# A softcap attention with a maxout layer behind it: another order in the hand-written list of work

## The chip, the cores and the metric

The kernel runs on one core of one Trainium2 chip. The core has five engines with a stream of instructions each: TensorE (PE, matmuls; its weight loads are a stream of their own, PEld), VectorE (DVE), ScalarE (ACT), GpSimd (POOL) and SyncE (SP). POOL and SP issue DMAs here. An engine runs its own instructions in order and waits for the others by semaphores. The metric is device microseconds for one execution; less is better. Several runs are made, and their median counts.

## The reference

```python
q, k, v: 8 x 12 x 448 x 64 (batch, heads, tokens, head size); cap = 30
scores = (q @ k^T) / 8
scores = cap * tanh(scores / cap)
attn = softmax(scores)                          # over the last axis
x = (attn @ v)  as rows of tokens: 3584 x 768
h1, h2 = x @ w1, x @ w2                         # w1, w2: 768 x 1024
out = maximum(h1, h2) @ w_out                   # w_out: 1024 x 768; out: 3584 x 768
```

## The kernel before

**What is computed.** No maximum is subtracted before the exponential, since tanh bounds the scores at 30; the scores are computed with k along the partitions, so that the exponents are already the operand of the matmul with v. The maxout layer is rewritten: max(h1, h2) @ w_out = relu(x (w1 − w2)) @ w_out + x (w2 w_out). `wd_sb` holds w1 − w2, `wm_sb` holds w2 w_out, and both are made at the start of each execution. All matmul operands are bf16.

**Units.** A pair `i` (0 to 47) is two heads, a quad `t` (0 to 23) is two pairs, so a batch is three quads. For a quad the steps are: transposed q and k (`X`/`XC` on PE and DVE for the first five quads; `cr t`, a DMA transpose that SP issues, L475, for the others), scores `S i j` (three blocks of keys, L509 to L514, two halves of 64 rows each), tanh `T i j` on ACT (L519), the left-over 64 keys `L`/`TL`/`EL`, exponents `E i j0 j1` on ACT (L536), sums of exponents `A` and `B` on DVE (L548, L553) and `Y` on PE, their inverse `Y1`, `Y2`, `Y3` on DVE, values `VL` and `V` on PE, and the normalisation `N t u` on DVE, which writes `xT` (u = 0 in one instruction, L618; u = 1 in two, L621).

**The layer.** It is computed in 120 groups, each one PSUM bank: `O g bank` opens a group, `M x y n` issues n pairs of half-matmuls (rows 0 to 63 for group x, rows 64 to 127 for group y), `M x x n` issues n full ones, `ev g` evicts it on DVE (relu, L666, or a copy, L702), and `eva g` does the copy on ACT (L700). A group has its two halves one after the other, and both add into the same bank. So between them stands a hand-over: `H g` puts a nop on DVE, `Hs g` puts it on SP (L652 to L655). The nop waits for the last half-matmul that the group had so far, and the first half-matmul of its other half waits for the nop (L646 to L648). `st b t` issues two output DMAs from SP (L676 to L681). POOL loads q, k, v and the weights (`lq`, `lk`, `lv`, `lw1`, `lw2`, `lwo`). `W`, `WC`, `P` and `PC` make `wm_sb`; `sub` makes `wd_sb`; `D` are matmuls that warm PE.

**The order.** It is a text, `ORDER` (lines 9 to 201): a list of steps that a loop at the end carries out one by one (L742 to L745). No scheduler moves anything, so each engine runs its instructions in the order in which the list issues them. The list decides nothing about time between engines: an instruction waits for what it reads, for buffers, and for what stands ahead of it on its engine.

**Buffers.** The transposed q and k have two buffers (`QB`), their rows two (`KB`). So `cr t` waits for the last scores of quad t − 2 as well as for its own loads: `cr 16`, say, writes the buffer of quad 14, whose last scores are `S 29 2`. The score tiles in PSUM are also reused: the values of a quad lie in one of them until `N` has read both parts.

Of the kernel before, what the change touches and what calls it, by code (L numbers as in the profile page):

```python
# [21 lines left out]
S 5 0; X 6 0; E 4 0 3; T 5 0; EL 2; Y1 1; Y2 1; PC 2 1; Y3 1; N 1 1; N 1 0; XC 6; X 7 2; W 4 1; S 5 2; S 5 1;
X 8 0; P 3 1 3; WC 4; XC 8; PC 3 1; T 5 1; T 5 2; OP 4 0 1; P 4 0 2; OP 0 1 0; P 0 1 3; S 6 0; S 6 1; W 5 3;
P 0 1 1; P 4 0 6; P 0 1 4; E 5 0 2; T 6 1; T 6 0; E 5 2 3; XC 7; sub 2 0; WC 5; sub 4 0; PC 4 0; sub 0 0; PC 0 1;
OP 5 1 3; P 5 1 4; S 6 2; L 3; Y 2 1; T 6 2; TL 3; E 6 0 3; VL 2; V 2 1 0 1; V 2 0 0 3; V 2 1 1 3; S 7 0; P 5 1 4;
OP 5 0 0; P 5 0 8; Y1 2; Y2 2; Y3 2; N 2 0; N 2 1; A 3 0 1; A 3 0 2; PC 5 1; PC 5 0; T 7 0; EL 3; lk 9 0; lq 11 0;
lv 3 1; lq 9 0; lw1 1; lw1 3; lq 10 0; lk 12 1; lv 3 0; lw1 5; lk 10 0; lk 11 0; lk 11 1; lk 10 1; S 7 2; O 0 1;
M 0 -1 2; S 7 1; M 0 -1 4; O 1 2; M 1 -1 1; T 7 2; T 7 1; Hs 0; M 1 -1 1; S 8 1; M 1 -1 1; M 1 0 3; S 8 0; X 9 3;
OP 4 1 0; P 4 1 4; sub 1 0; sub 3 0; XC 9; T 8 1; E 7 0 2; T 8 0; E 7 2 3; P 4 1 4; L 4; O 2 3; M 2 0 3; S 8 2;
M 2 1 3; A 3 1 1; B 3 1; PC 4 1; ev 0; B 3 0; Hs 2; TL 4; T 8 2; O 3 0; M 3 1 3; M 3 2 1; S 9 0; M 3 2 2; T 9 0;  # L30
E 8 0 3; ev 1; A 3 1 2; sub 5 0; cr 5; Hs 3; O 4 1; M 4 2 1; VL 3; V 3 0 0 3; Y 3 2; V 3 1 0 3; M 4 2 2; S 9 1;
M 4 3 3; lk 13 0; lk 13 1; lv 4 1; lv 4 0; lv 5 3; lv 5 0; lq 13 0; lq 15 0; lq 12 0; lk 12 0; lk 15 1; Y1 3;
Y2 3; Y3 3; ev 2; Hs 4; O 5 2; M 5 3 3; M 5 4 3; T 9 1; EL 4; ev 3; N 3 0; N 3 1; Hs 5; O 6 3; M 6 4 3; M 6 5 2;
# [172 lines left out]
def kernel(  # L206
# [21 lines left out]
    P = 128  # L228
# [550 lines left out]
```

## Time and profile before

| | before |
|---|---|
| median of 3 runs | 328.59 us |
| fastest and slowest run | 327.98 and 329.32 us |
| span of the profiled execution | 326.9 us |
| moved by DMA | 46.28 MB, 142 GB/s in the mean |
| TensorE clock granted | 0.9 or more in each of 40 slices |
| stores (SP), number and median to landing | 54, 4.5 us |

The profiled execution's span is 1.7 us under the median of the runs; it is counted from its first to its last instruction. In the profile, a row of the timeline is: start, duration, engine, line, operation, output and input names, and, in brackets, the idle time ahead of it and what ended it. An engine name with a q (SPq, DVEq) is the engine's own queue of waits and DMA issues. A nop of a hand-over shows as an EVENT_SEMAPHORE of L654.

### The profile page before, as it was taken

What the parts mean: (1) busy time and instruction counts of PE and PEld (TensorE: products, weight loads), DVE (VectorE), ACT (ScalarE), POOL (GpSimd) and SP (SyncE); (2) the same over time, 40 slices, a digit from 0 to 9 for tenths busy, and PEclk for the clock granted to TensorE, in tenths of its full rate; (3) what the DMA queues carried; (4) which work ended last, traced back from release to release, by engine and by line L of the source; (5) the groups of instructions that cost most, each with busy time, mean ns of one, the idle gap of its engine ahead of it and who ended that gap; (6) DMA issues with size and microseconds to landing.
All of it is one profiled execution on the core that took longest, in us unless ns stands there. A gap on an engine that the chain in (4) does not pass through costs nothing.

```text
span 326.9 us, 9772 instructions
## 1 busy us (share of the span) xinstructions
PE 320.2 (98%) x4138; PEld 184.5 (56%) x4138; DVE 240.1 (73%) x422; ACT 281.1 (86%) x278; POOL 162.2 (50%) x237
## 2 busy tenths in 40 slices
PE   7999999999999999999999999999999999999994
PEld 3454545545656664565565565556466556557662
DVE  3346899987997778987897788968878779773201
ACT  5999999999999999999999999999999999921120
POOL 7357584568772772764774474478448311000000
PEclk9999999999999999999999999999999999999999
DMA  8999999899999999999999999999999963013033
GB/s 179 174 202 185 269 256 112 92 140 116 221 188 98 134 182 191 102 99 175 163 176 108 208 114 181 128 140 182 183 116 101 201 156 45 2 50 98 0 98 96
DMA packets 134508, 46.28 MB, mean 142 GB/s; under 512 B 112321, under 2 KB 129473, under 8 KB 134465
## 3 DMA queue, kind: packets, MB, share of 16 engines
q0 software_dynamic: 94592, 25.02, 78.3%
q1 hardware_dynamic: 39424, 19.99, 31.1%
q8 instruction: 32, 0.52, 0.6%
q10 hardware_dynamic: 448, 0.66, 0.5%
q14 instruction: 12, 0.09, 0.1%
HBM read 47.78 MB, written 11.01 MB: 180 GB/s over the span
## 4 chain that ended last, share of the span: by engine, by line
PE 93%; DMA 3%; POOL 1%; DVE 1%; issue 0%
PE mm L645 61%; PE s L514 9%; PE s L606 9%; PE mm L431 5%; DMA w2b<-in_moe_w_dram 3%; PE s L528 2%; PE s L600 2%; PE mm L573 2%; PE mm L640 1%; POOL kqs L321 1%; PE mm L458 1%; PE mm L566 1%; PE mm L416 0%; DVE xT L621 0%; POOL w2b L366 0%; DVE xT L618 0%
## 5 line engine op out<-in xcount | busy, mean ns | idle before, releaser
L519 ACT ACTIVATE e<-s 128x896 bf16<-128x896 f32 x144 | 125.5, 927 | 5.7 <-PE s L514 5.2
L536 ACT ACTIVATE e<-e 128x1792 bf16<-128x1792 bf16 (+2 forms) x72 | 122.7, 1709 | 0.0
L645 PE MATMUL mm<-wo_sb,gT 64*128 64x384 bf16 x864 | 115.2, 323 | 0.0
L645 PE MATMUL mm<-wm_sb,xT 64*128 64x384 bf16 x648 | 102.2, 323 | 0.0
L645 PE MATMUL mm<-xT,wd_sb 64*128 64x448 bf16 x768 | 97.5, 349 | 0.0
L328 POOL DMA_DIRECT2D kqs<-in_k_dram x76 | 54.7, 722 | 56.1 <-DMA qkT<-kqs 50.9
L645 PEld LDWEIGHTS <-gT 64*128 64x128 bf16 x864 | 58.6, 94 | 25.5 <-issue 1.1
L645 PEld LDWEIGHTS <-wd_sb 64*128 64x128 bf16 x768 | 48.8, 94 | 26.7 <-issue 2.1
L645 PEld LDWEIGHTS <-xT 64*128 64x128 bf16 x648 | 50.3, 94 | 18.5 <-issue 0.2
L514 PE MATMUL s<-qkT 64*128 64x448 bf16 x288 | 52.7, 352 | 0.2 <-DVE xT L618 0.2
L352 POOL DMA_DIRECT2D vp<-in_v_dram x48 | 30.5, 639 | 32.6 <-PE s L514 23.5
L666 DVE TENSOR_SCALAR gT<-mm 128x448 bf16<-128x448 f32 x64 | 38.9, 617 | 8.7 <-PE mm L645 7.6
L328 POOL DMA_DIRECT2D kqs<-in_q_dram x38 | 35.1, 924 | 5.7 <-issue 2.5
L606 PE MATMUL s<-e,vp 128*32 128x448 bf16 x576 | 36.1, 354 | 0.0
L548 DVE TENSOR_TENSOR esum<-e 128x896 bf16<-128x896 bf16 x42 | 25.9, 617 | 9.1 <-ACT e L536 9.1
L621 DVE TENSOR_TENSOR xT<-s,inv 64x448 bf16<-64x448 f32 x48 | 29.9, 622 | 1.7 <-PE s L606 0.8
L548 DVE TENSOR_TENSOR esum<-esum,e 128x896 bf16<-128x896 bf16 x42 | 26.2, 623 | 5.9 <-ACT e L536 4.8
L514 PEld LDWEIGHTS <-qkT 64*128 64x128 bf16 x288 | 18.5, 94 | 20.1 <-issue 12.0
L700 ACT COPY osb<-mm 128x384 f32<-128x384 f32 x10 | 4.8, 479 | 26.9 <-PE mm L645 26.7
L702 DVE COPY osb<-mm 128x384 f32<-128x384 f32 x44 | 23.3, 554 | 6.2 <-PE mm L645 5.7
L553 DVE TENSOR_TENSOR esum<-esum,el 64x896 bf16<-64x896 bf16 x42 | 26.0, 619 | 1.2
L578 DVE STREAM_TRANSPOSE st<-mm 128x448 f32<-128x448 f32 x24 | 15.6, 649 | 13.0 <-PE mm L573 11.3
(57 smaller groups left out, 269.7 us busy)
## 6 DMA issues: line engine op xcount, KB each, us to landing
out_dram<-osb SPq DMA_DIRECT2D x54, 192.0 KB, 4.5
vp<-in_v_dram POOLq DMA_DIRECT2D x38, 160.0 KB, 4.3
kqs<-in_q_dram POOLq DMA_DIRECT2D x46, 112.0 KB, 5.8
kqs<-in_k_dram POOLq DMA_DIRECT2D x76, 56.0 KB, 4.4
osb<-in_moe_w_dram POOLq DMA_DIRECT2D x4, 512.0 KB, 7.4
w2b<-in_moe_w_dram POOLq DMA_DIRECT2D x6, 256.0 KB, 7.1
wo_sb<-in_moe_w_out_dram POOLq DMA_DIRECT2D x4, 384.0 KB, 9.9
vp<-in_v_dram POOLq DMA_DIRECT2D x10, 128.0 KB, 7.7
```

Source lines behind the costliest of these rows:

```text
L328: nc.gpsimd.dma_start(out=to, in_=x)
L352: nc.gpsimd.dma_start(out=to, in_=x)
L514: scored[i, j] = nc.tensor.matmul(s[:, h, :S], k_of(t, o, h, j), q_of(t, o, h)).ins
L519: nc.scalar.activation(expo[i][:, 2 * j : 2 * j + 2, :], slots[i, j][:, :, :S], AF.Tanh, scale=scale / cap)
L536: nc.scalar.activation(e, e, AF.Exp, scale=float(cap))
L548: nc.vector.tensor_add(d, e[:, 0:2, :] if j == 1 else d, e[:, 2 * j : 2 * j + 2, :])
L553: nc.vector.tensor_add(d, d, left_e[t][r, :, :])
L606: nc.tensor.matmul(vals[t][place(m, u), u, :S], w[:, m, :], expo[2 * t + o][:, 2 * j + h, :], start=False, stop=(j == NJ - 1))
L621: nc.vector.tensor_mul(x[64 - r : 128 - r], vals[t][r : r + 64, u, :S], sums[t, 3][64 - r : 128 - r])
L645: ins = nc.tensor.matmul(self.ps, w[r], x[r], start=first, stop=self.at == [self.n, self.n]).ins
L666: nc.vector.tensor_relu(gT[b // 2][:, f, cs], ps)
L702: nc.vector.tensor_copy(o[:, hs], ps)
```

## The change

The text `ORDER` is written anew. The work is the same but for two evictions, and a line of code gets another condition that has the same effect for this list:

```diff
-        if c != 1:
+        if bank is not None:
             turned["qk", i] = mm_tile(bank).bitcast(bf16)
```

Two evictions, of groups 22 and 25, go from DVE to ACT (`ev` to `eva`), and some hand-overs go from SP to DVE or back. The warming matmuls `D` are placed otherwise, with the same number in sum, and a few groups open other banks. PE's order is the same up to `S 1 0` and, but for small swaps, from `S 19 0` on. The pieces below are those where the order on SP, DVE or ACT changes beside hand-overs; the numbers after a group in `Hs 54 2` are not used by the code.

The third quad's normalisation, with an add between its parts, and the start of the layer:

```diff
-OP 5 0 0; P 5 0 8; Y1 2; Y2 2; Y3 2; N 2 0; N 2 1; A 3 0 1; A 3 0 2; PC 5 1; PC 5 0; T 7 0; EL 3; lk 9 0; lq 11 0;
...
-M 0 -1 2; S 7 1; M 0 -1 4; O 1 2; M 1 -1 1; T 7 2; T 7 1; Hs 0; M 1 -1 1; S 8 1; M 1 -1 1; M 1 0 3; S 8 0; X 9 3;
...
+V 2 0 0 3; E 6 0 3; Y2 2; V 2 1 1 3; Y3 2; S 7 0; N 2 1; P 5 1 1; OP 5 0 3; P 5 0 3; P 5 1 3; T 7 0; P 5 0 1;
+A 3 0 1; P 5 1 1; P 5 0 3; N 2 0; EL 3; P 5 0 1; S 7 1; O 0 2; M 0 -1 1; A 3 0 2; M 0 -1 1; T 7 1; S 7 2;
```

Evictions 22 and 25, and the transpose of quad 10:

```diff
-M 25 24 2; lv 9 3; M 25 24 2; EL 8; M 25 24 1; S 17 1; lk 22 1; M 25 24 2; ev 22; M 25 24 1; T 17 1; S 17 2;
...
-M 24 25 4; lq 23 0; M 24 25 3; T 18 0; O 27 0; M 27 25 1; A 8 1 1; M 27 25 1; cr 10; M 27 25 1; M 27 26 1; ev 24;
-M 27 26 1; T 18 1; M 27 26 1; S 18 2; ev 25; M 27 26 2; T 18 2; M 27 26 1; B 8 0; M 27 26 4; B 8 1; st 1 3;
...
+eva 22; M 25 24 1; lk 22 1; M 25 24 1; A 8 0 1; M 25 24 1; T 17 1; S 17 2; M 25 24 1; ev 23; M 25 24 1; lq 22 0;
+cr 10; M 25 24 1; T 17 2; M 25 24 2; S 18 0; M 25 24 1; lk 23 0; O 26 3; M 26 24 1; T 18 0; M 26 24 1; H 25;
+M 26 24 1; Hs 24; M 26 25 2; lk 23 1; M 26 25 1; E 17 0 2; M 24 25 1; S 18 2; Hs 26; M 24 25 1; lq 23 0; S 18 1;
+M 24 25 6; T 18 1; O 27 0; M 27 25 1; A 8 1 1; M 27 25 2; M 27 26 1; ev 24; M 27 26 1; eva 25; M 27 26 2; B 8 0;
```

The hand-over of group 38 goes from DVE to SP (that of group 68, beside `cr 18`, in the same way):

```diff
-O 38 2; M 38 36 1; A 10 1 1; M 38 36 1; Hs 37; cr 12; M 38 36 1; T 22 1; M 38 37 1; S 22 2; B 10 0; M 38 37 2;
-T 22 2; O 39 0; M 39 37 1; ev 36; M 39 37 2; H 38; B 10 1; E 21 2 3; M 39 38 3; ev 37; L 11; VL 10; TL 11;
...
+O 38 2; M 38 36 2; A 10 1 1; Hs 37; cr 12; M 38 36 1; T 22 1; M 38 37 1; S 22 2; B 10 0; M 38 37 2; T 22 2;
+O 39 0; M 39 37 1; ev 36; M 39 37 2; E 21 2 3; Hs 38; B 10 1; M 39 38 3; ev 37; L 11; VL 10; TL 11; A 10 1 2;
```

The hand-over of group 52 goes from SP to DVE (that of group 82 in the same way), and `cr 15` moves up:

```diff
-M 52 51 1; O 53 1; M 53 51 1; A 13 0 2; M 53 51 1; Hs 52; lq 33 0; M 53 51 1; M 53 52 2; ev 51; M 53 52 1; T 28 0;
...
+T 27 2; O 52 3; M 52 50 2; Hs 51; cr 15; lq 32 0; A 13 0 1; M 52 50 1; M 52 51 1; E 27 0 2; M 52 51 1; ev 50;
+S 28 1; M 52 51 1; lk 33 0; O 53 1; M 53 51 1; A 13 0 2; M 53 51 2; lk 33 1; H 52; ev 51; M 53 52 1; T 28 0;
```

`cr 16` moves ahead of the hand-over of group 55 (`cr 22` ahead of that of group 85, in the same way):

```diff
-M 55 54 2; ev 52; M 55 54 1; T 29 1; S 29 2; lq 34 0; M 55 54 1; ev 53; M 55 54 1; O 56 3; M 56 54 1; T 29 2;
-M 56 54 1; A 14 0 1; Hs 55; S 30 0; M 56 54 1; lk 35 0; M 56 55 1; A 14 0 2; M 56 55 1; Hs 54 2; E 29 0 2;
-M 56 55 1; S 30 1; lk 35 1; M 54 55 1; Hs 56; M 54 55 4; lq 35 0; M 54 55 3; T 30 0; O 57 1; M 57 55 1; A 14 1 1;
-M 57 55 1; cr 16; M 57 55 1; M 57 56 1; ev 54; M 57 56 1; T 30 1; M 57 56 1; S 30 2; ev 55; M 57 56 2; T 30 2;
...
+lk 34 1; S 29 2; M 55 54 1; ev 53; M 55 54 1; cr 16; O 56 3; M 56 54 1; lq 34 0; T 29 2; M 56 54 1; Hs 55;
+S 30 0; A 14 0 1; M 56 54 1; M 56 55 2; E 29 0 2; Hs 54; A 14 0 2; M 56 55 1; lk 35 0; S 30 1; M 54 55 3;
```

`cr 21` moves ahead of the hand-overs of groups 81 and 82:

```diff
-ev 78; M 81 80 1; S 39 2; S 40 0; ev 79; M 81 80 1; T 39 2; O 82 3; M 82 80 1; lk 45 0; M 82 80 1; A 19 0 1;
-Hs 81; M 82 80 1; M 82 81 1; E 39 0 2; M 82 81 1; lk 45 1; ev 80; S 40 1; M 82 81 1; O 83 2; M 83 81 1; A 19 0 2;
...
+S 40 0; M 81 80 1; ev 79; T 39 2; cr 21; O 82 3; M 82 80 1; lk 45 0; M 82 80 1; Hs 81; M 82 80 1; A 19 0 1;
```

`cr 17` moves ahead of the hand-over of group 59 (`cr 11` and `cr 23` ahead of those of 29 and 89, in the same way):

```diff
-T 31 2; M 59 58 1; A 15 0 1; S 32 0; M 59 58 2; A 15 0 2; M 59 58 1; lk 37 0; E 31 0 2; O 60 3; M 60 58 1; S 32 1;
-M 60 58 1; Hs 59; M 60 58 1; lk 37 1; M 60 59 2; Hs 58 2; M 60 59 1; M 58 59 1; lq 37 0; M 58 59 1; T 32 0; Hs 60;
-M 58 59 1; A 15 1 1; M 58 59 1; cr 17; M 58 59 2; B 15 0; M 58 59 1; T 32 1; M 58 59 1; S 32 2; O 61 1; M 61 59 1;
...
+S 31 1; lk 36 1; M 59 58 3; T 31 1; ev 56; S 31 2; lq 36 0; M 59 58 1; ev 57; M 59 58 1; cr 17; M 59 58 1;
+T 31 2; M 59 58 1; A 15 0 1; S 32 0; M 59 58 1; lk 37 0; M 59 58 2; E 31 0 2; A 15 0 2; O 60 3; M 60 58 1;
+S 32 1; lk 37 1; M 60 58 1; Hs 59; M 60 58 1; M 60 59 2; lq 37 0; Hs 58; st 3 5; M 60 59 1; M 58 59 2; T 32 0;
```

Stores in the tail, ahead of the hand-overs of groups 102 and 105:

```diff
-M 103 102 2; eva 101; M 103 102 1; N 23 0; M 103 102 3; N 23 1; M 103 102 5; O 104 3; M 104 102 3; Hs 103;
-M 104 103 2; Hs 102 2; M 104 103 1; M 102 103 2; Hs 104; M 102 103 4; st 6 1; M 102 103 2; O 105 0; M 105 103 2;
...
-M 108 106 2; Hs 107; M 108 106 1; M 108 107 2; ev 106; st 6 2; M 108 107 1; O 109 0; M 109 107 2; H 108;
...
+Hs 103; st 6 1; M 104 102 1; M 104 103 2; Hs 102; M 104 103 1; M 102 103 3; Hs 104; M 102 103 5; O 105 0;
+M 105 103 2; eva 102; M 105 103 1; M 105 104 2; eva 103; M 105 104 1; O 106 1; M 106 104 2; st 6 2; Hs 105;
```

More of the change, by code (lines that the diff above doesn't have):

```diff
@@ new lines @@
+VL 0; lk 8 0; XC 4; V 0 1 0 3; E 2 0 3; Y2 0; lq 8 0; V 0 0 0 3; Y3 0; lq 7 0; OP 0 0 1; P 0 0 1; N 0 0;
+P 0 0 1; lw2 4; P 0 0 1; OP 2 1 0; P 2 1 2; lv 6 2; N 0 1; P 2 1 1; OP 1 1 2; P 1 1 1; P 2 1 1; E 3 0 2;
+P 0 0 1; lq 6 0; P 1 1 2; P 0 0 1; lk 7 0; P 1 1 1; S 3 2; S 4 0; lk 6 0; P 0 0 1; T 3 2; P 0 0 1; lw2 5;
+P 2 0 1; P 1 1 2; PC 2 0; P 2 1 1; lw1 2; T 4 0; P 1 1 2; P 0 0 1; P 2 1 1; lw1 4; E 3 2 3; PC 0 0; S 4 1;
+S 4 2; X 5 3; lw1 0; T 4 1; Y 1 1; XC 5; lv 2 0; T 4 2; PC 1 1; L 2; lv 2 1; Y1 1; P 2 1 1; OP 3 1 3; P 3 1 1;
@@ new lines @@
+M 10 11 4; lk 17 0; E 11 2 3; M 10 11 3; lk 16 0; L 6; ev 10; VL 5; TL 6; V 5 1 0 2; H 12; A 5 1 2; lk 17 1;
+V 5 1 2 3; V 5 0 0 2; E 12 0 3; lq 17 0; Y 5 3; V 5 0 2 3; Y1 5; O 13 2; M 13 11 3; lv 7 0; M 13 12 1; Y2 5;
+M 13 12 1; S 13 0; Y3 5; lv 7 1; M 13 12 4; N 5 0; lv 7 2; M 13 12 1; T 13 0; M 13 12 3; N 5 1; lv 7 3;
+M 13 12 1; EL 6; O 14 3; M 14 12 2; Hs 13; st 0 0; S 13 1; M 14 12 1; M 14 13 1; T 13 1; M 14 13 1; H 12; ev 11;
+S 13 2; M 14 13 1; M 12 13 1; T 13 2; M 12 13 1; H 14; A 6 0 1; M 12 13 4; A 6 0 2; E 13 0 2; M 12 13 2;
@@ new lines @@
+M 28 29 1; A 9 1 1; M 28 29 4; T 20 1; B 9 0; M 28 29 2; S 20 2; O 31 0; M 31 29 1; Hs 30; B 9 1; M 31 29 1;
+ev 28; M 31 29 1; M 31 30 1; T 20 2; M 31 30 1; ev 29; M 31 30 1; O 32 1; M 32 30 2; H 31; st 1 6; M 32 30 1;
+E 19 2 3; L 10; ev 30; VL 9; V 9 0 0 2; TL 10; A 9 1 2; V 9 1 0 2; E 20 0 3; M 32 31 1; Y 9 3; V 9 0 2 3;
+V 9 1 2 3; lk 26 0; Y1 9; S 21 0; M 32 31 2; Y2 9; lv 11 0; O 33 3; M 33 31 1; Y3 9; M 33 31 1; Hs 32;
+M 33 31 1; lv 11 1; M 33 32 2; T 21 0; N 9 0; M 33 32 1; O 34 2; M 34 32 1; lv 11 2; M 34 32 1; Hs 33; ev 31;
@@ new lines @@
+M 41 40 1; ev 39; S 24 1; M 41 40 1; lv 12 3; M 41 40 3; lk 28 1; M 41 40 1; st 2 0; M 41 40 3; T 24 0;
+M 41 40 1; A 11 1 1; lq 28 0; O 42 2; M 42 40 3; H 41; T 24 1; B 11 0; M 42 41 1; S 24 2; H 40; lk 29 0;
+M 42 41 2; B 11 1; M 40 41 1; T 24 2; M 40 41 1; lk 29 1; M 40 41 4; E 23 2 3; M 40 41 1; lq 29 0; M 40 41 1;
+O 43 0; M 43 41 1; ev 40; L 12; VL 11; A 11 1 2; TL 12; V 11 0 0 2; V 11 1 0 2; E 24 0 3; Y 11 3; V 11 0 2 3;
+V 11 1 2 3; Y1 11; S 25 0; M 43 41 2; Y2 11; M 43 42 2; Y3 11; M 43 42 4; N 11 0; M 43 42 2; T 25 0; M 43 42 2;
@@ new lines @@
+ev 44; T 26 2; M 47 45 1; lk 31 1; M 47 45 1; H 46; B 12 1; M 47 46 1; E 25 2 3; M 47 46 1; lq 31 0; st 2 2;
+M 47 46 1; ev 45; O 48 3; M 48 46 1; L 13; VL 12; A 12 1 2; TL 13; V 12 0 0 2; V 12 1 0 2; E 26 0 3; Y 12 1;
+V 12 0 2 3; V 12 1 2 3; Y1 12; S 27 0; lv 14 0; M 48 46 2; Y2 12; M 48 47 1; Y3 12; M 48 47 1; lv 14 1;
+M 48 47 1; O 49 1; M 49 47 2; Hs 48; ev 46; lv 14 2; M 49 47 1; T 27 0; M 49 48 2; N 12 0; lv 14 3; M 49 48 1;
+O 50 2; M 50 48 2; EL 13; Hs 49; ev 47; M 50 48 1; S 27 1; M 50 49 1; N 12 1; M 50 49 1; T 27 1; M 50 49 1;
@@ new lines @@
+lk 35 1; M 54 55 2; Hs 56; M 54 55 1; st 3 3; M 54 55 1; lq 35 0; M 54 55 1; T 30 0; O 57 1; M 57 55 1;
+A 14 1 1; M 57 55 2; M 57 56 1; ev 54; M 57 56 1; T 30 1; M 57 56 1; S 30 2; ev 55; M 57 56 2; T 30 2;
+M 57 56 1; B 14 0; M 57 56 1; st 3 4; M 57 56 3; B 14 1; E 29 2 3; M 57 56 1; O 58 2; M 58 56 2; L 15; VL 14;
+A 14 1 2; TL 15; V 14 0 0 2; V 14 1 0 2; E 30 0 3; Y 14 0; V 14 0 2 3; lk 36 0; V 14 1 2 3; Y1 14; S 31 0;
+M 58 56 1; M 58 57 1; lv 16 0; Y2 14; M 58 57 1; Hs 56; M 58 57 1; Y3 14; M 56 57 2; lv 16 1; Hs 58; M 56 57 2;
@@ new lines @@
+Hs 64; M 65 63 1; M 65 64 1; ev 62; lq 38 0; S 33 2; S 34 0; M 65 64 1; T 33 2; ev 63; M 65 64 1; O 66 2;
+M 66 64 1; lk 39 0; M 66 64 1; A 16 0 1; Hs 65; M 66 64 1; E 33 0 2; M 66 65 1; S 34 1; ev 64; lk 39 1;
+M 66 65 2; O 67 3; M 67 65 1; A 16 0 2; M 67 65 1; Hs 66; lq 39 0; M 67 65 1; M 67 66 1; T 34 0; M 67 66 1;
+ev 65; M 67 66 1; O 68 0; M 68 66 2; A 16 1 1; Hs 67; cr 18; M 68 66 1; T 34 1; M 68 67 1; S 34 2; B 16 0;
+M 68 67 2; T 34 2; O 69 1; M 69 67 1; ev 66; M 69 67 2; E 33 2 3; Hs 68; B 16 1; M 69 68 3; ev 67; L 17; VL 16;
@@ new lines @@
+M 89 88 3; T 43 1; ev 86; S 43 2; M 89 88 2; ev 87; cr 23; M 89 88 1; T 43 2; M 89 88 1; S 44 0; A 21 0 1;
+M 89 88 3; E 43 0 2; A 21 0 2; O 90 3; M 90 88 1; S 44 1; M 90 88 1; Hs 89; M 90 88 1; M 90 89 2; Hs 88;
+M 90 89 1; st 5 5; M 88 89 2; T 44 0; M 88 89 1; A 21 1 1; M 88 89 4; T 44 1; B 21 0; M 88 89 1; Hs 90; S 44 2;
+O 91 2; M 91 89 1; ev 88; M 91 89 1; T 44 2; M 91 89 1; M 91 90 1; B 21 1; M 91 90 2; E 43 2 3; O 92 0;
+M 92 90 1; ev 89; M 92 90 1; H 91; M 92 90 1; L 22; st 5 6; ev 90; VL 21; TL 22; V 21 0 0 2; A 21 1 2;
@@ new lines @@
+M 97 95 1; A 22 0 2; M 97 95 1; Hs 96; M 97 95 1; M 97 96 1; T 46 0; M 97 96 1; ev 95; M 97 96 1; O 98 1;
+M 98 96 2; A 22 1 1; Hs 97; M 98 96 1; T 46 1; M 98 97 1; S 46 2; B 22 0; M 98 97 2; T 46 2; O 99 2; M 99 97 1;
+ev 96; M 99 97 1; Hs 98; M 99 97 1; M 99 98 1; E 45 2 3; B 22 1; M 99 98 3; L 23; ev 97; VL 22; TL 23;
+V 22 0 0 2; A 22 1 2; V 22 1 0 2; E 46 0 3; Y 22 0; V 22 0 2 3; V 22 1 2 3; Y1 22; S 47 0; M 99 98 2; Y2 22;
+M 99 98 2; Y3 22; M 99 98 3; O 100 3; M 100 98 1; N 22 0; M 100 98 1; Hs 99; T 47 0; M 100 98 1; M 100 99 2;
@@ new lines @@
+N 22 1; Hs 98; M 100 99 1; M 98 99 1; EL 23; M 98 99 2; S 47 1; M 98 99 2; T 47 1; M 98 99 1; Hs 100; A 23 0 1;
+S 47 2; M 98 99 2; O 101 0; M 101 99 1; A 23 0 2; T 47 2; M 101 99 2; M 101 100 1; ev 98; M 101 100 2; E 47 0 2;
+M 101 100 1; ev 99; M 101 100 4; st 6 0; M 101 100 3; O 102 1; M 102 100 2; E 47 2 3; Hs 101; M 102 100 1;
+A 23 1 1; M 102 101 3; Hs 100; B 23 0; VL 23; V 23 0 0 2; B 23 1; V 23 1 0 2; M 100 101 1; A 23 1 2;
+M 100 101 4; Y 23 2; V 23 0 2 3; V 23 1 2 3; Y1 23; M 100 101 3; Y2 23; O 103 2; M 103 101 2; Y3 23; eva 100;
@@ new lines @@
+M 103 101 1; M 103 102 2; eva 101; M 103 102 1; N 23 0; M 103 102 4; N 23 1; M 103 102 4; O 104 3; M 104 102 2;
+Hs 103; st 6 1; M 104 102 1; M 104 103 2; Hs 102; M 104 103 1; M 102 103 3; Hs 104; M 102 103 5; O 105 0;
+M 105 103 2; eva 102; M 105 103 1; M 105 104 2; eva 103; M 105 104 1; O 106 1; M 106 104 2; st 6 2; Hs 105;
+M 106 104 1; M 106 105 2; ev 104; M 106 105 1; O 107 2; M 107 105 3; Hs 106; M 107 106 2; ev 105; M 107 106 1;
+O 108 3; M 108 106 2; Hs 107; M 108 106 1; M 108 107 2; ev 106; M 108 107 1; O 109 0; M 109 107 2; H 108;
```

291 lines of the change are left out of this document (123 added, 168 removed).

## The prediction

> **What bounds the kernel now.** The page comes first: span, busy shares, the 40 slices, the chain that ended last. Then the view of waits, for TensorE (PE) and ScalarE (ACT).
>
> ```profile
> span 326.9 us, 9772 instructions
> PE 320.2 (98%) x4138; PEld 184.5 (56%) x4138; DVE 240.1 (73%) x422; ACT 281.1 (86%) x278; POOL 162.2 (50%) x237
> ...
> PE   7999999999999999999999999999999999999994
> ...
> ACT  5999999999999999999999999999999999921120
> ...
> PE 93%; DMA 3%; POOL 1%; DVE 1%; issue 0%
> ```
> ```profile
> PE mm L471 <- DVE warm L734: 1.8, 1, 1.8
> PE mm L416 <- DMA w2b<-in_moe_w_dram: 0.5, 1, 0.5
> PE s L514 <- DVE xT L618: 0.2, 1, 0.2
> ...
> ACT e L519 <- PE s L514: 5.2, 9, 0.8
> ```
>
> PE is busy in every slice but the ends, and holds 93% of the chain. Its three waits are 2.5 us in all, the last under 0.5 us behind the start. ACT, the next busiest, waits 5.2 us for scores and is done by the 35th slice; behind that PE is nearly alone with matmuls. So an instruction that PE waits for, anywhere from 50 us on, moves the end by its whole length, and nothing behind it can win the time back: there are no PE waits left to absorb it. The multiset of matmuls is the same in both lists, and the count of changes of matmul shape along PE's order falls from 82 to 81 in the part that differs; PE's own work is therefore priced at nothing, and what the change can do lies in waits.
>
> Where can such a wait arise? A matmul group is fed in halves (rows 0 to 63, rows 64 to 127), and two groups swap halves by a hand-over: a nop on SyncE (SP, `Hs`) or VectorE (DVE, `H`) that waits for the last matmul of one half; the next half's first matmul waits for the nop. SP also issues the transposes (`cr`) and the stores (`st`), in list order. The next rows are one place where before has a transpose near such a nop.
>
> ```profile
> L475 SPq DMA_TRANSPOSE qkT<-kqs x19: 1296/1655/2655, 55.3 to 262.6; - x19
> ...
> 55.25 1.58 SPq L475 DMA_TRANSPOSE qkT<-kqs  x1
> ...
> 55.69 0.75 PE L645 MATMUL mm<-xT,wd_sb 64*128 64x448 bf16 x6
> ...
> L654 SPq EVENT_SEMAPHORE  x1: 17/17/17, 56.9 to 56.9; - x1
> ```
>
> The nop could have run soon after its half ended (that half lies in the row from 55.69; its last start is some 55.9). It ran at 56.9, right behind 55.25 + 1.58 = 56.83. So the transpose occupies SP for its whole duration, 1.30 to 2.65 us, median 1.66, and a nop behind it waits. Here the released half stands behind more matmuls of values, so PE lost nothing. Nowhere in before's list does a transpose stand shortly ahead of a hand-over whose half comes soon. How close a hand-over can run is seen at group 52:
>
> ```profile
> L654 DVEq EVENT_SEMAPHORE  x1: 21/21/21, 171.5 to 171.5; - x1
> ...
> 171.59 0.49 PE L645 MATMUL mm<-wm_sb,xT 64*128 64x384 bf16 x2
> ```
>
> The half starts 0.1 us behind its nop, with no wait listed. I take 0.15 us from the end of whatever holds SP to the released matmul: 0.05 for the nop (56.9 behind 56.83), 0.1 for this gap.
>
> **The change part by part.** The terms are sums on before's own times: when SP gets to the nop in the new order, against when before's PE started the half.
>
> **A. `Hs 38` and `Hs 68` right behind `cr 12` and `cr 18`.** Before has these two hand-overs on DVE. Behind the waiting nop stand only later SP steps; PE waits for it.
>
> ```profile
> 134.69 1.69 SPq L475 DMA_TRANSPOSE qkT<-kqs  x1
> ...
> 136.03 0.75 PE L645 MATMUL mm<-wm_sb,xT 64*128 64x384 bf16 x5
> ```
>
> 134.69 + 1.66 + 0.15 = 136.50 against 136.03: 0.47 us, twice, 0.94. With 1.30 it is 0.11 each, with 2.65 it is 1.46 each.
>
> **B. `cr 16` and `cr 22` now ahead of `Hs 55` and `Hs 85`.** The transpose writes a buffer that the last scores of an earlier quad read (two buffers), so it starts when `S 29 2` is done; in before it stood after three more nops.
>
> ```profile
> 177.43 0.35 PE L514 MATMUL s<-qkT 64*128 64x448 bf16 x2
> ...
> 178.62 0.67 PE L645 MATMUL mm<-wm_sb,xT 64*128 64x384 bf16 x6
> ```
>
> The scores end at 177.78; 177.78 + 1.66 + 0.15 = 179.59 against 178.62: 0.97 each, 1.94 for the two (0.61 to 1.96 each). `Hs 54` and `Hs 56` queue behind `Hs 55`, but their halves are later by the same stall.
>
> **C. `cr 21` ahead of `Hs 81`**, and no longer behind `Hs 82`.
>
> ```profile
> 236.67 0.54 PE L514 MATMUL s<-qkT 64*128 64x448 bf16 x4
> ...
> 237.81 0.35 PE L645 MATMUL mm<-xT,wd_sb 64*128 64x448 bf16 x1
> ```
>
> The first pair of these four is `S 39 2`, done at 236.67 + 0.35 = 237.02. 237.02 + 1.66 + 0.15 = 238.83 against 237.81: 1.02 (0.66 to 2.01).
>
> **D. `cr 10`, `cr 11`, `cr 17`, `cr 23` moved ahead of `Hs 24`, `Hs 29`, `Hs 59`, `Hs 89`.** Nearly clear, by the example of `cr 17`:
>
> ```profile
> 188.92 0.35 PE L514 MATMUL s<-qkT 64*128 64x448 bf16 x2
> ...
> 191.19 0.35 PE L645 MATMUL mm<-xT,wd_sb 64*128 64x448 bf16 x1
> ```
>
> 189.27 + 1.66 + 0.15 = 191.08 against 191.19: nothing at the median, 0.88 with 2.65. Some of the 19 are over 1.77, so I take 0.1 each, 0.4 (0 to 3.5).
>
> The Trainium skill, "DMA: Bandwidth & Descriptors", section "Issuing engines are not separate DMA queues", says that the time on the sequencer to initiate a DMA is usually small relative to the DMA itself. If that held for SP here, A to D would all be nothing; the rows above put the hold at 1.30 us at the least, so the sum goes by the rows.
>
> **E. Stores ahead of hand-overs in the tail.** `st 6 1` now stands between `Hs 103` and `Hs 102`, `st 6 2` ahead of `Hs 105`. Each issues two DMAs from SP.
>
> ```profile
> L654 SPq EVENT_SEMAPHORE  x1: 17/17/17, 292.7 to 292.7; - x1
> ...
> 293.44 0.32 PE L645 MATMUL mm<-wm_sb,xT 64*128 64x384 bf16 x1
> ...
> 293.92 1.11 SPq L681 DMA_DIRECT2D out_dram<-osb  x2
> ...
> 295.10 1.05 ACT L700 COPY osb<-mm 128x384 f32<-128x384 f32 x2 [3.73 <-PE mm L645]
> ...
> L654 SPq EVENT_SEMAPHORE  x1: 17/17/17, 296.2 to 296.2; - x1
> ```
>
> `Hs 103` runs at 292.7, the stores take 1.11: 292.7 + 1.11 + 0.15 = 293.96 against 293.44 for the half that `Hs 102` releases, 0.52. `st 6 2` waits for the second ACT copy, 295.10 + 1.05 = 296.15; plus 1.11, the nop of `Hs 105` comes at 297.3 where it was at 296.2; the half has up to 0.3 to spare, so 0.8 to 1.1, taken as 0.85. Together 1.4. If the stores held SP no time, 0; if one pair took twice 1.11, 2.5.
>
> **F. `H 52` and `H 82` on DVE behind `A 13 0 2`, `A 19 0 2`;** before has them on SP.
>
> ```profile
> 168.22 0.61 DVE L548 TENSOR_TENSOR esum<-esum,e 128x896 bf16<-128x896 bf16 x1
> ...
> 168.72 0.56 PE L645 MATMUL mm<-wm_sb,xT 64*128 64x384 bf16 x4
> ```
>
> 168.83 + 0.1 = 168.93 against 168.72: 0.2 each. The add waits for ACT's exponents, and ACT gains on a stalled PE, so DVE may be ahead by then: 0.3 for both (0 to 0.5).
>
> **G. The early part.** Third quad's second half is normalised first, one `A` slips between the halves, ACT takes two evictions from DVE (`eva 22`, `eva 25`), some tanh and exponents swap places.
>
> ```profile
> 45.98 0.62 DVE L618 TENSOR_TENSOR xT<-s,inv 128x448 bf16<-128x448 f32 x1
> ...
> 46.61 1.26 DVE L621 TENSOR_TENSOR xT<-s,inv 64x448 bf16<-64x448 f32 x2
> 47.79 0.61 DVE L548 TENSOR_TENSOR esum<-e 128x896 bf16<-128x896 bf16 x1
> ...
> L700 ACT COPY osb<-mm 128x384 f32<-128x384 f32 x10 | 4.8, 479 | 26.9 <-PE mm L645 26.7
> ...
> 21.04 1.73 ACT L519 ACTIVATE e<-s 128x896 bf16<-128x896 f32 x2 [0.44 <-PE s L514]
> ...
> 96.40 0.92 ACT L519 ACTIVATE e<-s 128x896 bf16<-128x896 f32 x1 [0.73 <-PE s L514]
> ```
>
> Both halves are done 0.61 later with the add between them (1.26 + 0.61 + 0.62 in place of 0.62 + 1.26), and PE already waited 0.2 for this step; scores that reuse the tile come later by up to that, though PE has premultiplied weights (`P`) moved there. ACT gets 2 × 0.48 = 0.96 of copies, near the place where it idled 0.73 at 96.40. I take +0.4; bounds −0.7 (both PE waits of 0.5 and 0.2 gone) and +1.6 (0.61 and 0.96 paid in full). The other hand-overs that change engine, and the stores that move up beside the scores, stand with several other matmuls ahead of the half that the next nop releases, and cost nothing; without that cover each store would cost as E does.
>
> Sum: 0.94 + 1.94 + 1.02 + 0.4 + 1.4 + 0.3 + 0.4 = 6.4 us, all on PE. The span goes from 326.9 to 333.3. The median of the runs, 328.59, stands 1.7 above the profiled span; 328.59 + 6.4 = 335.0. The low ends add to 0.22 + 1.22 + 0.66 + 0 + 0.5 + 0 − 0.7 = 1.9 (E with half its hold), 330.5.
>
> **The rivals.** *SP is free at once.* If the nop at 56.9 was late for another reason (a semaphore that arrived late), A to E vanish and F and G stay: 328.59 + 0.7 = 329.3, no measurable change. For it: no PE wait in before shows the price. Against it: the nop lies 0.07 behind the transpose's end, and the profile books SP 1.30 us or more for every one of 19. Its chance is 0.11; the skill's sentence quoted above would come out here.
>
> *ACT's order sets the pace, and the change is faster.* ACT is at 86% and all of its 5.2 us are waits for scores that PE computes in list order; if ACT's early gaps of 0.44 and 0.73 close and PE's 0.7 go, with SP's holds covered by the lead, the kernel gains 0.44 + 0.73 + 0.7 = 1.9: 326.7. Against it: PE has no waits on ACT to give back, and matmuls alone fill the tail. 0.05.
>
> *Long transposes.* With the new places the transposes issue earlier, while loads still run; if those holds are near the longest, 2.65, A to D are 2.92 + 3.92 + 2.01 + 3.5 = 12.4, and the sum 12.4 + 1.4 + 0.7 = 14.5: 343.1. It decides where a transpose waits for its own load besides the scores. For it: the maximum was seen once; against it, the median is 1.66. 0.06.
>
> **How the numbers follow.** The forecast (PE stalls at some eight hand-overs) has 0.78. A measurement of this kernel tells about 0.5%, 1.6 us, from no change (326.9 to 330.2). Faster is the second rival, 0.05; same the first, 0.11; slower the forecast and the third, 0.84. The forecast's own range is 330.5 to 340; reaching down to the first rival's 329.3, a little below it, and up to 341 leaves about 2 in 10 out.
>
> **What would show it.** In the profile after, the view of waits lists PE waiting on SP nops at the hand-overs of groups 38, 68, 55, 85 and 81, by about 0.5, 0.5, 1, 1 and 1 us, and in the tail at 102 and 105; the nop's start lies 0.1 behind the end of a transpose or a store. The part up to 115 us ends within 1 us of before. ACT's waits grow by about what PE loses. I am wrong if these nops run during a transpose, if PE's waits stay near 2.5 us, or if the loss lies ahead of 115 us.

## The result, and the profile after

The changed kernel takes 333.32 us (median of 4 runs, 332.90 to 334.05) against 328.28 us in the same comparison (4 runs): a ratio of 1.0152, 95% interval 1.0131 to 1.0173. It is 5.0 us slower; 6.4 were forecast. The profiled execution's span went from 326.9 to 331.6 us, by 4.7. First the page, then the view of waits (in us: total, number, longest) and the view of the hand-over nops, with those that waited for them:

```profile
span 331.6 us, 9776 instructions
PE 321.7 (97%) x4138; PEld 184.7 (56%) x4138; DVE 240.1 (72%) x420; ACT 281.8 (85%) x280; POOL 161.6 (49%) x237
...
PE 94%; ACT 2%; SPq 1%; issue 1%; DVE 0%
```
```profile
PE mm L651 <- SPq L660: 3.0, 6, 0.8
PE mm L477 <- DVE warm L740: 1.8, 1, 1.8
...
PE s L520 <- ACT e L525: 0.4, 1, 0.4
...
ACT e L525 <- PE s L520: 6.5, 10, 1.0
```
```profile
L660 SPq EVENT_SEMAPHORE  x106: 17/17/17, 50.0 to 320.6; - x106
L660 DVEq EVENT_SEMAPHORE  x28: 21/21/21, 52.2 to 304.0; - x28
...
  PEld L651: 6.3, 9
  PE mm L651: 3.0, 6
```

(The code's lines are six further down: L660 is L654 of before, L651 is L645, L481 is L475.) A row that before did not have stands at the top: PE waits for nops on SP, six times, 3.0 us, and the weight loads, which come first, nine times, 6.3 us. No DVE nop is waited for. Here are the places in the timeline (groups 38, 55, 68, 81, 85, 102 and 105, in this order); each SP row is followed by the released half-matmul, with the idle time of PE in brackets:

```profile
134.77 1.89 SPq L481 DMA_TRANSPOSE qkT<-kqs  x1
136.78 0.50 PE L651 MATMUL mm<-wm_sb,xT 64*128 64x384 bf16 x4 [0.39 <-SPq L660]
...
178.23 1.57 SPq L481 DMA_TRANSPOSE qkT<-kqs  x1
179.91 0.66 PE L651 MATMUL mm<-wm_sb,xT 64*128 64x384 bf16 x5 [0.56 <-SPq L660]
...
206.30 1.30 SPq L481 DMA_TRANSPOSE qkT<-kqs  x1
207.71 0.53 PE L651 MATMUL mm<-wm_sb,xT 64*128 64x384 bf16 x4
...
238.35 1.48 SPq L481 DMA_TRANSPOSE qkT<-kqs  x1
239.94 0.36 PE L651 MATMUL mm<-xT,wd_sb 64*128 64x448 bf16 x1 [0.60 <-SPq L660]
...
250.29 1.76 SPq L481 DMA_TRANSPOSE qkT<-kqs  x1
252.17 0.66 PE L651 MATMUL mm<-wm_sb,xT 64*128 64x384 bf16 x5 [0.75 <-SPq L660]
...
296.07 1.10 SPq L687 DMA_DIRECT2D out_dram<-osb  x2
297.29 0.33 PE L651 MATMUL mm<-wo_sb,gT 64*128 64x384 bf16 x1 [0.24 <-SPq L660]
...
299.88 1.11 SPq L687 DMA_DIRECT2D out_dram<-osb  x2
301.09 1.12 PE L651 MATMUL mm<-xT,wd_sb 64*128 64x448 bf16 x10 [0.44 <-SPq L660]
```

Every released half starts 0.10 to 0.12 us behind the end of a transpose or of a pair of stores: 134.77 + 1.89 = 136.66 and 136.78; 178.23 + 1.57 = 179.80 and 179.91; 299.88 + 1.11 = 300.99 and 301.09. Before had these halves earlier behind their groups' last matmuls; what they follow now is SP. The time for which such a row occupies SP is called its hold below.

Where the time goes is read best from lags: the start of one and the same half-matmul, the last one ahead of a hand-over, in a trace, minus its start in before's trace. Along a row, a lag changes only where time is lost or won. Its first value says little, since executions with the very same early list differ there by up to 0.8 us. About 0.5 us of that is a single early wait that the other executions lack (0.52 us for `w2b` at 15.20 in before, 0.47 at 35.59 after). "28b" and so on is the second hand-over of that group.

| lag in us at group | 28b | 37 | 39 | 56b | 80 | 83 | 88 | 103 | 104 | 106 |
|---|---|---|---|---|---|---|---|---|---|---|
| after | −0.08 | +0.09 | +0.40 | +1.29 | +1.28 | +2.13 | +3.20 | +3.29 | +3.29 | +4.51 |

The steps are at the places of the terms: +0.31 at group 38 (A), +0.87 and +1.07 at 55 and 85 (B), +0.84 at 81 (C), +1.22 at 102 and 105 (E). Ahead of that stand −0.31 at 115 us, a wait of +0.23 at group 26 behind stores, and +0.17 at 124 to 127 us; behind it +0.2 up to the end. With these the steps add to the span's 4.7. The view's 3.0 us of waits are less than the steps: a wait is counted only from the end of the last matmul's row, and at each place but group 38 it is 0.24 to 0.32 us shorter than the step.

### The profile page after: what moved, and what is told of

The parts are those of the page before. It is cut to its first block, busy times and chain, and to the rows that moved or that the text cites. A ratio compares the mean times of both kernels' runs of the same rounds, so it can differ in the third digit from the quotient of the medians.

```text
span 331.6 us, 9776 instructions
## 1 busy us (share of the span) xinstructions
PE 321.7 (97%) x4138; PEld 184.7 (56%) x4138; DVE 240.1 (72%) x420; ACT 281.8 (85%) x280; POOL 161.6 (49%) x237
## 4 chain that ended last, share of the span: by engine, by line
PE 94%; ACT 2%; SPq 1%; issue 1%; DVE 0%
PE mm L651 60%; PE s L520 9%; PE s L612 9%; PE mm L437 5%; PE s L534 2%; PE s L606 2%; PE mm L579 2%; PE mm L464 1%; PE mm L646 1%; ACT e L525 1%; PE mm L477 1%; PE mm L422 1%; ACT e L542 1%; SPq L481 1%; SPq L687 1%; PE mm L572 1%
## 5 line engine op out<-in xcount | busy, mean ns | idle before, releaser
L651 PE MATMUL mm<-wo_sb,gT 64*128 64x384 bf16 x864 | 117.1, 323 | 0.3 <-SPq L660 0.2
L651 PE MATMUL mm<-wm_sb,xT 64*128 64x384 bf16 x648 | 105.4, 323 | 1.7 <-SPq L660 1.7
L651 PE MATMUL mm<-xT,wd_sb 64*128 64x448 bf16 x768 | 99.2, 349 | 1.0 <-SPq L660 1.0
L651 PEld LDWEIGHTS <-gT 64*128 64x128 bf16 x864 | 59.9, 94 | 25.1 <-SPq L660 1.1
L651 PEld LDWEIGHTS <-wd_sb 64*128 64x128 bf16 x768 | 48.0, 94 | 29.1 <-issue 2.1
L651 PEld LDWEIGHTS <-xT 64*128 64x128 bf16 x648 | 50.6, 94 | 21.9 <-SPq L660 3.3
L612 PE MATMUL s<-e,vp 128*32 128x448 bf16 x576 | 35.2, 354 | 0.0
L706 ACT COPY osb<-mm 128x384 f32<-128x384 f32 x12 | 5.8, 482 | 28.5 <-PE mm L651 28.2
L708 DVE COPY osb<-mm 128x384 f32<-128x384 f32 x42 | 22.5, 555 | 5.4 <-PE mm L651 4.8
L538 ACT ACTIVATE el<-s 128x896 bf16<-128x896 f32 x24 | 22.3, 929 | 2.8 <-PE s L534 2.3
```

Source lines behind the costliest of these rows:

```text
L612: nc.tensor.matmul(vals[t][place(m, u), u, :S], w[:, m, :], expo[2 * t + o][:, 2 * j + h, :], start=False, stop=(j == NJ - 1))
L651: ins = nc.tensor.matmul(self.ps, w[r], x[r], start=first, stop=self.at == [self.n, self.n]).ins
L708: nc.vector.tensor_copy(o[:, hs], ps)
```

## The experiments

The runs of before that go with the experiments have a median of 328.53 us (14 runs, first four experiments) and 328.39 us (23 runs, last four).

**The nops away from SP.** The changed list, and nothing moved but thirteen nops:

```diff
-O 39 0; M 39 37 1; ev 36; M 39 37 2; E 21 2 3; Hs 38; B 10 1; M 39 38 3;
+O 39 0; M 39 37 1; ev 36; M 39 37 2; E 21 2 3; H 38; B 10 1; M 39 38 3;
```

(the same for the first hand-overs of groups 54, 55, 59, 68, 81, 84, 85, 89, 101, 102 and 105, and the second of 26)

> The changed list with thirteen hand-over nops that stand on SP behind a transpose or a store (groups 26, 38, 68, 55, 54, 85, 84, 81, 59, 89, 101, 102, 105) put on DVE; transposes and stores stay in their new places. Theory (SP is held, and only the nops behind it suffer): no PE wait on SP nops, and the lags that the two traces show at these places, 0.2 + 0.3 + 0.9 + 1.1 + 0.8 + 0.1 + 0.5 + 0.7 = 4.6 us, go: 333.3 - 4.6 = 328.7, span 327.0. Rival 1 (the new places of transposes and stores disturb the rest by their traffic, or the new order of PE and ACT is the dearer): 333.3 as before. Rival 2 (DVE is as busy at these places as SP is held): about half comes back, 331, with waits on DVE nops.

Measured: 328.48 us (10 runs), ratio to before 1.0001 (0.9991 to 1.0010). All of the loss is gone, with transposes and stores in their new places. The nops' view and a transpose in the timeline:

```profile
L653 SPq EVENT_SEMAPHORE  x93: 17/17/17, 49.2 to 315.2; - x93
L653 DVEq EVENT_SEMAPHORE  x41: 21/21/21, 51.4 to 299.0; - x41
its engine sat idle before it (us, times) until:
who waited for it (us, times):
busy tenths in 40 slices 0000000000000000000000000000000000000000
```
```profile
176.89 1.57 SPq L474 DMA_TRANSPOSE qkT<-kqs  x1
```

The list under "who waited" is empty: nobody waits for a nop any more, though quad 16's transpose takes the same 1.57 us in the same place. (The lags of this run still grow by 0.44 from group 28 to the end, 0.16 of it at 124 to 127 us and 0.27 at 258.5 us, where no hand-over stands and scores come late behind a normalisation on DVE; whether the nops put there delayed it was not tried.) So the loss is neither the transposes' traffic nor the new order of PE and ACT (rival 1), nor is DVE as bad a place as SP (rival 2).

**Only the three transposes moved back.**

```diff
-... ev 53; M 55 54 1; cr 16; O 56 3; ...
+... ev 53; M 55 54 1; O 56 3; ... Hs 56; cr 16; M 54 55 1; ...
```

(the same for `cr 22` behind `Hs 86`, and `cr 21` from ahead of `O 82 3` to behind `H 82`)

> The changed list with only three transposes moved back behind the hand-overs: quad 16 behind that of group 56, quad 22 behind that of group 86, quad 21 behind that of group 82; all nops as changed. Theory: the lags of the terms B and C, 0.87 + 1.07 + 0.84 = 2.8 us, go: 333.3 - 2.8 = 330.5; those at groups 38, 102 and 105 stay. Rival (the early transposes themselves cost nothing, the order of PE does): 333.3. Rival (a later transpose comes too late for its quad's scores): PE waits for the transposed q and k, and less than 2.8 comes back.

Measured: 330.19 us (5 runs), ratio 1.0058 (1.0038 to 1.0078), so 3.1 us under the changed kernel. Its waits:

```profile
PE mm L644 <- SPq L653: 1.1, 4, 0.4
```

The 3.0 us are now 1.1, and no wait for transposed q and k has come. Lags in the table below: nothing is lost from group 39 to 56b, and 0.4 from there to 83, all of it between groups 59 and 62, behind `cr 17`.

**Only the two stores of the tail moved back.**

```diff
-Hs 103; st 6 1; M 104 102 1; M 104 103 2; Hs 102; M 104 103 1; M 102 103 3; Hs 104; M 102 103 5;
+Hs 103; M 104 102 1; M 104 103 2; Hs 102; M 104 103 1; M 102 103 3; Hs 104; st 6 1; M 102 103 5;
```

(and `st 6 2` from ahead of `Hs 105` to behind `Hs 107`)

> The changed list with only the two stores of the tail moved back (t = 1 of batch 6 behind the hand-over of group 104, t = 2 behind that of group 107). Theory: the lags at groups 102 and 105, 0.52 + 0.70 = 1.2 us, go: 333.3 - 1.2 = 332.1. Rival (the tail is set by ACT's evictions of groups 102 and 103, which a store only waits for): 333.3.

Measured: 332.41 us (4 runs, 331.00 to 333.05), ratio 1.0111 (1.0083 to 1.0139): 0.9 under the changed kernel, which these few runs alone don't separate well. The lag does: it is +2.31 at groups 103, 104 and 106, where the changed kernel goes from 3.29 to 4.51.

```profile
PE mm L644 <- SPq L653: 2.2, 4, 0.8
```

**The three transposes alone, in the list of before.** (They leave their old places, `cr 16` behind `M 57 55 1`, say.)

```diff
-... ev 53; M 55 54 1; O 56 3; M 56 54 1; T 29 2; ...
+... ev 53; M 55 54 1; cr 16; O 56 3; M 56 54 1; T 29 2; ...
```

(the same for `cr 22` behind `ev 83; M 85 84 1`, and `cr 21` behind `T 39 2`)

> The list of before with only three transposes moved ahead, to the places of the changed list: quad 16 ahead of the hand-over of group 55, quad 22 of group 85, quad 21 of group 81. Theory: + 2.8 us alone (0.87 + 1.07 + 0.84): 328.3 + 2.8 = 331.1, with three PE waits on SP nops of 0.7 to 1 us. Rival (a sum over many small moves, none of which costs by itself): 328.3.

Measured: 332.42 us (4 runs), ratio 1.0116 (1.0101 to 1.0131): +3.9, where 2.8 were expected. Three moves by themselves cost most of what the whole change costs, though with longer holds. Waits and timeline:

```profile
PE mm L642 <- SPq L651: 3.4, 3, 1.6
```
```profile
177.35 2.64 SPq L472 DMA_TRANSPOSE qkT<-kqs  x1
180.10 0.66 PE L642 MATMUL mm<-wm_sb,xT 64*128 64x384 bf16 x5 [1.62 <-SPq L651]
...
250.52 1.87 SPq L472 DMA_TRANSPOSE qkT<-kqs  x1
252.81 0.66 PE L642 MATMUL mm<-wm_sb,xT 64*128 64x384 bf16 x5 [1.16 <-SPq L651]
```

By the lags the three moves cost 4.3 us here, 1.5 over the 2.8. Most of the surplus is the length of one transpose: quad 16's took 2.64 us here and 1.57 in the changed kernel, 1.07 more, and the lag at that place grows by 1.94 in place of 0.87, also 1.07 more. There SP's hold is the end's delay, microsecond for microsecond. Another 0.4 came at group 85: the half starts 0.42 us behind the end of the transpose's row, not 0.11, since the nop itself ran 0.36 us behind that end. What held SP there is open.

**The hand-overs of 38 and 68 alone, in the list of before.**

```diff
-T 22 2; O 39 0; M 39 37 1; ev 36; M 39 37 2; H 38; B 10 1; E 21 2 3;
+T 22 2; O 39 0; M 39 37 1; ev 36; M 39 37 2; Hs 38; B 10 1; E 21 2 3;
...
-T 34 2; O 69 1; M 69 67 1; ev 66; M 69 67 2; H 68; B 16 1; E 33 2 3;
+T 34 2; O 69 1; M 69 67 1; ev 66; M 69 67 2; Hs 68; B 16 1; E 33 2 3;
```

> The list of before with only the hand-overs of groups 38 and 68 put from DVE to SP, behind the transposes of quads 12 and 18. Theory (the wait is what is left of the transpose's hold at the moment the half is due): 0.1 to 1.5 us each by the length that the transpose happens to take, 0.3 + 0.8 with before's lengths of 1.69 and 2.27, 0.3 + 0 with the changed kernel's 1.89 and 1.30: 328.6 to 329.6. Rival (SP is free once the DMA is issued): 328.3, no PE wait at either.

Measured: 328.62 us (10 runs), ratio 1.0005 (0.9991 to 1.0019). That can't be told from no change, nor the theory's 328.6 from the rival's 328.3; the trace has to decide. The timeline and the nops' view:

```profile
134.00 1.51 SPq L472 DMA_TRANSPOSE qkT<-kqs  x1
135.62 0.66 PE L642 MATMUL mm<-wm_sb,xT 64*128 64x384 bf16 x5
...
204.33 1.32 SPq L472 DMA_TRANSPOSE qkT<-kqs  x1
```
```profile
  PEld L642: 0.7, 2
```

SP is not free: the half starts at 135.62, 0.11 behind 134.00 + 1.51. But it starts only 0.28 us later after its group's last half-matmul than in before (1.09 against 0.81), and the lag stays at −0.69. The half has some 0.35 us to spare here: in the changed kernel it was 0.65 late and cost 0.31; in the run with the transposes moved back, 0.55 late and cost 0.20. This spare time the forecast lacked. With it, the holds of 1.51 and 1.32 us cost nothing here.

**The early part alone.** The changed list up to the scores of pair 19, before's list from there (the first `M 28 26` behind the joint counted anew).

```diff
 ... Y1 8; S 19 0;
-lv 10 0; M 28 26 2; Y2 8; M 28 27 2; Y3 8; Hs 26; lv 10 1; ...
+M 28 26 2; M 28 27 1; Y2 8; M 28 27 1; Hs 26 2; lv 10 0; M 28 27 1; Y3 8; ...
```

> The changed list up to the scores of pair 19 (115 us), the list of before from there on. Theory (term G has the other sign from the forecast's: the early part gains the 0.3 us that the traces show at 115 us, apart from the wait at group 26): 328.3 - 0.3 = 328.0, no difference that can be measured, span 326.6, PE 0.3 us ahead of before at 120 us. Forecast's own term: + 0.4, 328.7. Rival (the early part costs something that is paid later, where ACT has to catch up): over 329.

Measured: 328.66 us (12 runs), ratio 1.0006 (0.9990 to 1.0021), so between 0.3 us less and 0.7 us more than before. The time tells no difference. The traces tell one in a stretch: from the first hand-over of the layer (group 0) to the first of group 28, three executions with before's early list take 66.54 to 66.55 us, and five with the changed one 65.86 to 65.87; up to group 0 the changed one is 0.2 later in the mean (49.05 against 48.87), where executions of one list differ by 0.7 to 0.8. By the traces about half a microsecond is won. The runs don't bear that out: they scatter by two, and the profiled execution is the fastest of the twelve (327.62). Whether the early part wins or loses stays open.

```profile
span 325.8 us, 9776 instructions
```

**Each transpose issued in two halves,** in the changed list:

```diff
-        nc.sync.dma_start_transpose(out=qkT_of(t), in_=kqs[t % KB].rearrange("p j c -> p (j c)"))
+        for h in range(2):
+            js = slice(h * R7, (h + 1) * R7)
+            nc.sync.dma_start_transpose(out=qkT_of(t)[:, js, :], in_=kqs[t % KB][:, js, :].rearrange("p j c -> p (j c)"))
```

> The changed list with each transpose issued as two DMAs of half the size, k then q. If SP's hold is a price per byte (per tile moved), two halves hold it as long as one, and the time stays at 333.3. If it is mostly a price per instruction, the hold nearly doubles, to about 3 us, and B and C lose 1.5 us more each, A 1.5 each, D up to 1 each: about 333.3 + 10 = 343. If SP waits for the data to land, each half would take the 4 to 8 us that the landing takes, and far more is lost.

Measured: 342.27 us (4 runs), ratio 1.0435 (1.0397 to 1.0473): 9 us more than the changed kernel. The transposes' and the waits' rows:

```profile
L483 SPq DMA_TRANSPOSE qkT<-kqs x38: 1222/1274/2103, 55.1 to 270.7; - x38
```
```profile
PE mm L653 <- SPq L662: 10.4, 11, 1.8
```

Half a transpose holds SP for 1.22 to 2.10 us, median 1.27; a whole one 1.30 to 2.64, median 1.58. So half the size still takes four fifths of the hold, by the medians, and most of it is a price per instruction: the two halves of a quad hold SP for 2.61 us in the median (their sum, 19 quads), 1.65 times as long as a whole. All of D now counts too: the hand-overs of 24, 29, 59 and 89 wait.

**The transposes on ACT,** in the changed list: `nc.sync` becomes `nc.scalar` in that line.

> The changed list with all transposes issued by ACT in place of SP. Theory (the issuing engine's sequencer is held, whichever it is): no PE wait on SP nops at groups 38, 55, 81, 85, but ACT is held about 1.6 us 19 times, 30 us on 282 us busy; it also waits there for the scores of an earlier quad. PE then waits for tanh and exponents: slower than 333.3. Rival (the hold belongs to the DMA's traffic, or to SP alone): ACT's instructions show no gaps behind the transposes, and the stalls either stay (333.3) or go (329).

Measured: 357.32 us (4 runs), ratio 1.0871 (1.0836 to 1.0906). The transposes' row, two of PE's waits, and one place on ACT:

```profile
L481 ACTq DMA_TRANSPOSE qkT<-kqs x19: 1312/1870/4805, 54.7 to 286.8; - x19
```
```profile
PE s L520 <- ACT e L525: 18.6, 14, 3.2
...
PE mm L651 <- SPq L660: 0.7, 2, 0.4
```
```profile
115.58 2.18 ACTq L481 DMA_TRANSPOSE qkT<-kqs  x1
117.80 1.73 ACT L525 ACTIVATE e<-s 128x896 bf16<-128x896 f32 x2 [2.14 <-DMA kqs<-in_q_dram]
```

The hold goes with the issuing engine: ACT's next tanh starts 0.04 behind the transpose's end (115.58 + 2.18 = 117.76), and behind 16 of the 19 transposes ACT's next operation starts 0.05 us behind the end, as counted in the trace; at the other three an operation was still running. The stalls on SP nops shrink from six to two, and PE waits 18.6 us for ACT instead. Not all of that is the hold; ACT also waits at these places for loads and for the scores that the transpose must follow, and the run doesn't part these.

The lags of these runs, in the manner of the table above:

| lag in us at group | 28b | 37 | 39 | 56b | 83 | 88 | 103 | 106 |
|---|---|---|---|---|---|---|---|---|
| nops on DVE | −1.09 | −0.93 | −0.92 | −0.92 | −0.93 | −0.92 | −0.65 | −0.65 |
| three transposes back | −0.95 | −0.78 | −0.58 | −0.54 | −0.19 | −0.18 | −0.09 | +1.13 |
| two stores back | −0.96 | −0.78 | −0.71 | +0.30 | +1.13 | +2.21 | +2.31 | +2.31 |
| before, three transposes | −0.47 | −0.47 | −0.47 | +1.47 | +2.37 | +3.85 | +3.85 | +3.85 |
| before, nops 38 and 68 | −0.69 | −0.69 | −0.69 | −0.68 | −0.69 | −0.68 | −0.67 | −0.67 |
| early part alone | −1.08 | −1.08 | −1.08 | −1.07 | −1.08 | −1.07 | −1.07 | −1.07 |
| transposes halved | +0.18 | +1.06 | +1.97 | +4.02 | +7.72 | +9.72 | +10.79 | +12.01 |

No run beats before by anything that can be measured: PE has no waits left there behind 37 us, and all that the experiments can do is add none.

## Why the prediction was right

The sign, the mechanism and most places were right; the sum was 1.4 us over the timed difference and 1.7 over the span's. That it came no further off is in part luck: the terms that were too large (A, C, D, E, F and G) were some 2 us too large together, and about 0.7 us was lost at places without a term. By its steps:

- **PE bounds, and a stall goes to the end in full.** Shown: the lags never shrink behind a stall by more than 0.2 us, and the excess length of one transpose came out at the end one to one. Two readings on the way were wrong and carried nothing: the last of before's three PE waits lies at 36.55 us, not within 0.5 of the start, and by the two traces the changes of matmul shape (rows and columns) rise from 131 to 132 over the whole program, where a fall by one was said.
- **SP is held by a transpose for its whole duration.** Shown from three sides: nops moved off SP (all comes back), halved transposes (a quad's hold grows to 1.65 times, the waits from 3.0 to 10.4 us), another issuing engine (the hold moves). The Trainium skill, "DMA: Bandwidth & Descriptors", section "Issuing engines are not separate DMA queues", calls the time to initiate a DMA usually small relative to the DMA. The view of the transposes after has both (ns min, median and max of the hold; us to landing):

```profile
L481 SPq DMA_TRANSPOSE qkT<-kqs x19: 1295/1581/2635, 55.7 to 262.8; - x19
...
DMA to landing us min/median/max: 3.8/5.9/7.9
```

  A transpose holds SP for 1.58 us in the median; from issue to landing it takes 5.9. So the trace agrees as far as 27% is called small. What counts here is another time, from a group's last half-matmul to the half that it releases: 0.6 to 0.9 us at the stalled places in before, and the hold is longer than that. The first rival, which rested on an idle SP, is refuted.
- **B**, forecast 1.94, measured 0.87 + 1.07 = 1.94. The mechanism is shown, the equal sum is luck: the two holds, 1.57 and 1.76, happen to average the 1.66 that was put in, and the same two moves in the list of before cost 1.94 + 1.48. **C**, 1.02 and 0.84. **E**, 1.4 and 0.52 + 0.70 = 1.22.
- **A** was mis-sized: 0.94 forecast, 0.31 measured. The step "against when before's PE started the half" took that start as the latest that costs nothing; the half of group 38 had 0.35 us more. With quad 18's transpose at 1.30, the shortest, the hand-over of 68 cost nothing.
- **D**, 0.4 forecast as an allowance: the lag returns to 1.28 behind group 62, so nothing in the changed kernel, though `cr 17` cost 0.4 in the run with the three transposes moved back, where it held SP for 2.28 us and not 1.88. A place like these that the forecast passed over cost 0.23: the second hand-over of group 26 behind stores. One store held SP for 1.26 us there; in the runs with transposes or stores moved back it took 0.61 and 0.64, and nothing was lost:

```profile
114.50 1.26 SPq L683 DMA_DIRECT2D out_dram<-osb  x1
```

- **F** failed: 0.3 forecast, nothing measured, for a reason of its own (last section).
- **G** stays open: +0.4 forecast, about −0.5 in the traces, −0.3 to +0.7 in the times. In the changed kernel the steps behind 115 us alone add to 5.0, the timed difference, which leaves about nothing for G. One reading was wrong: the 0.2 us that PE waited for `xT` in before was taken for the third quad's step, whose first half runs at 45.98, but it lies at 36.55, behind a half of the second quad:

```profile
36.55 0.55 PE L514 MATMUL s<-qkT 64*128 64x448 bf16 x4 [0.16 <-DVE xT L618]
```

  In the new order that wait is gone, and one of 0.4 us for ACT is there instead, at 14.29. Which of the early swaps wins or loses was not tried.
- **Signs named in advance.** PE waits at 38, 55, 85, 81, 102 and 105, as said, by 0.2 to 0.8 us; at 68 not. The part up to 115 us ends within 1 us of before, as said (−0.31). ACT's waits for scores grew by 1.3 us, from 5.2 to 6.5, not by what PE lost.

The other two rivals: ACT as the pace-setter fell with the first experiment, where ACT's new order stays and nothing is gained; the long transposes did not come, since the holds at the places of A, B and C were 1.30 to 1.89, but one shows in the experiment where quad 16's took 2.64.

## What to carry to other kernels

Where one engine is busy all the time, go through the instructions that it waits for and ask what stands ahead of each on the queue that issues it; an idle engine that only issues DMAs can be held long enough to stall the busy one. Put short signals on a queue that has no DMA issue ahead of them, or put the DMA issues behind the signals that are due soon. And give each such signal its spare time from the trace before pricing a delay: the first tenths of a microsecond may be free.

## What the runs showed of the hardware

A nop on DVE does not wait for the vector operation ahead of it to end. In the changed kernel the nop of group 52 stands right behind an add in DVE's order, and it ran while the add did:

```profile
168.63 0.62 DVE L554 TENSOR_TENSOR esum<-esum,e 128x896 bf16<-128x896 bf16 x1
```
```profile
L660 DVEq EVENT_SEMAPHORE  x1: 21/21/21, 168.7 to 168.7; - x1
```

The add runs from 168.63 to 169.25, the nop at 168.7. In the run with nops on DVE, at least 27 of the 41 ran inside another DVE operation. That is why term F cost nothing and why DVE, busy 72%, was a good place for nops where SP, which does little, was not: on SP, the DMA's issue itself occupies the queue.

The length of a whole transpose's hold on SP varies between 1.30 and 2.99 us over the eight traces that have it. Some places vary between executions (quad 18's took 2.27 in before, and 1.30 in the run where only quads 16, 21 and 22 had moved), others hardly do (quad 13's took 1.30 to 1.31 in all eight). What sets it was not tried.
